# Pairing two early softmax tiles of an attention and MLP kernel: when their exponentials run

## The chip, the cores and the metric

The kernel runs on one core of one Trainium2 chip. The metric is the device time of one execution in microseconds (us); less is better. The time before is 385.89 us, the median of 3 runs (385.85 to 385.94).

The engines named below are PE (TensorE, matrix products; PEld is its load of weights), DVE (VectorE), ACT (ScalarE), POOL (GpSimd) and SP (SyncE, which here does nothing but issue DMAs). Each engine takes its instructions strictly in the order in which the program gives them, so an instruction that waits holds up all that stand behind it on its engine.

## The reference

One transformer block over 2048 positions of width 576: an attention in which each position looks at itself and at seven earlier positions two apart, with 32 heads of 18 channels, and a two-layer MLP with 4608 hidden channels. Both have a layer norm ahead and a residual behind.

```python
def _A_ref(x, wqkv, wo):                       # H = 32, Dh = 18, W = 8, dil = 2
    qkv = (x @ wqkv).reshape(B, S, 3, H, Dh)   # then transposed to q, k, v
    idx = pos[:, None] - off[None, :]          # off = 0, 2, ..., 14
    mask = idx >= 0
    logits = jnp.einsum("bhsd,bhswd->bhsw", q, kg) * scale
    logits = jnp.where(mask[None, None, :, :], logits, -1e9)
    attn = _softmax(logits, axis=-1)
    o = jnp.einsum("bhsw,bhswd->bhsd", attn, vg)
    return o.transpose(0, 2, 1, 3).reshape(B, S, D) @ wo
def _B_ref(x, w1, b1, w2, b2):
    y = _layernorm(x, axis=-1)
    h = _gelu(jnp.einsum("bsd,df->bsf", y, w1) + b1)   # tanh form
    return jnp.einsum("bsf,fd->bsd", h, w2) + b2
x = A_x
h = x + _A_ref(_layernorm(x, axis=-1), A_wqkv, A_wo)
h2 = h + _B_ref(_layernorm(h, axis=-1), B_w1, B_b1, B_w2, B_b2)
return h2
```

## The kernel before

**Tiles and groups.** The 2048 positions are cut into 16 tiles of 128 (numbers n = 0 to 15). Two neighbouring tiles make a group (g = 0 to 7): the MLP runs a group at a time, the attention a tile at a time. In this text "tile 2" is n = 2, the third tile.

**A list scheduler in Python sets the order.** Every piece of work is a task with an engine, an estimated cost, the tasks it comes after, a priority and, where it needs one, a buffer slot (class Weaver, L16). `run()` keeps an estimated clock for each engine and takes, again and again, the ready task with the earliest estimated start; among tasks with the same start the lower priority number goes first (L58). An engine's instruction order is the order in which its tasks are taken; it is fixed before the kernel runs. Loads on SP also carry an estimate of the DMA queue: 240 KB per us (L33), and a task that waits for a load starts, in the plan, at that landing. A change to one dependency can therefore move any task behind it, on all engines.

**The tasks of one tile**, with the names that the prediction uses:

- `c{n}Q/K/V` (PE, L392): the three projections, each 10 matmuls; `e{n}Q/K/V` (ACT, L405): their eviction from PSUM. K and V go into one slot of an eight-slot window (`kwin`, `vwin`); even and odd positions have a window each.
- `p1a`, `p1s`, `p1t`, `p1b` (DVE, L444, L450, L457 to L463), together the logits of a tile: q times the K window, a tree of adds, then maximum and subtraction. The tile's product uses the single buffer `prod`.
- `ex{n}` (ACT, L467): the exponential over the tile's logits, in place.
- `p2n` (DVE, L437 to L439, L475, L478): the sum, its reciprocal and the weights; `p2a`, `p2s`, `p2b` (DVE, L485, L491, L495 to L497): the weights times the V window and a tree of adds. `p2a` uses `prod` too.
- `ks{n}`, `vs{n}` (SP, L519, L521): once tile n's logits (or its product with V) have read the window, one slot of K (of V) is loaded again from DRAM, shifted by one row, for the next tile. `p1a` of a tile waits for the `ks` of all earlier tiles of its parity, `p2a` for their `vs`.
- `t2{n}`: the transposes of the attention's output. For tiles 0 to 2 they are nine PE transposes into a PSUM buffer (`t2p`, L321) and a copy by ACT (L538); from tile 3 on two DMA transposes (L540, L541).
- `wo{n}` (PE, L563): the output projection; `woe{n}` (ACT, L568): its eviction; `xr{n}` (SP, L572): the residual is loaded.
- `ln2a`, `hb` (DVE, L576, L306, L307, L310, L589): residual, statistics of the second layer norm, and the residual plus the last bias; `ln2r` (POOL, L314): the reciprocal root; `ln2m` (DVE, L584); `ln2b` (ACT, L593): the normalized tile; `t3{n}`: its transposes into `hnT`, by PE and ACT or by DMA in the same way as `t2`.

**The MLP of group g** is a row of nine units. `u{g}.{u}` (PE, L629) is 36 matmuls into one PSUM buffer `pm`; `g{g}.{u}` (ACT, L640) is the four gelus that empty it. After the row `m{g}.…` (PE, L666) multiplies by w2 in four passes, and `out` (DVE, L685) adds the residual. A unit of row g comes after both `t3` of its group and after the last `m` of the group before.

**PSUM.** There are three `pm` buffers. Projections, PE transposes, output projections and units of all rows share them; each is free again when ACT has emptied it.

**ACT's tables.** Exponential and gelu use different activation tables; a table load (ACT_TABLE_LOAD) stands in the program wherever one follows the other. Copies, casts and `Identity` do not bring a load about.

**Where the exponentials stand before.** For tiles 6 to 15 (groups 3 to 7) both tiles of a group get their logits first; both exponentials come after that and after the last gelu of the group two before, and ahead of the first gelu of the group before (L509, L651). For tiles 0 to 5 each exponential comes after its own tile's logits and may fall anywhere. Logits of tile 4 and later may start once the logits of the tile before are done; those of tiles 1, 2 and 3 wait until the tile before is through with its product with V (L501).

Of the kernel before, what the change touches and what calls it, by code (L numbers as in the profile page):

```python
# [15 lines left out]
class Weaver:  # L16
# [9 lines left out]
    def add(self, name, engine, cost, fn, after=(), prio=0.0, take=None, give=(), lag=0.1, table=None, kb=0.0,  # L26
            backlog=2.5, transfers=1):
        assert name not in self.tasks, name
        self.tasks[name] = (engine, cost, fn, tuple(after), prio, take, tuple(give), lag, table,
                            (kb, backlog, transfers))  # L30
# [60 lines left out]
def kernel(  # L91
# [33 lines left out]
    GROUPS = [[n, n + 1] for n in range(0, NT, 2)]  # L125
# [47 lines left out]
    add = wv.add  # L173
# [41 lines left out]
    UN = FH // 2  # L215
# [19 lines left out]
    Q, K, V = 0, 1, 2  # L235
# [194 lines left out]
    def attention(n):  # L430
        j = ORDER[n]
        e, s = j % 2, j // 2
# [60 lines left out]
        def p2b():  # L493
# [4 lines left out]
                                    op=ALU.add)  # L498

        ready = [f"e{m}K" for m in same] + [f"ks{m}" for m in before]  # L500
        add(f"p1a{n}", "DVE", 2.65, p1a, ready + [f"e{n}Q"] + [f"lg{n}"] + ([f"p2b{n - 1}"] if 0 < n < 4 else [f"p1b{n - 1}"] if n else []), prio=n,  # L501
            take=("prod", f"prod{n}"), give=(f"q{n}",))
        add(f"lg{n}", "-", 0.0, lambda: None, [f"lg{n - 1}"] if n else [], take=("lg", f"lg{n}"), lag=0.0)
        add(f"p1s{n}", "DVE", 1.37, lambda: p1b(((9, 18),)), (f"p1a{n}",), prio=n)
# [1 line left out]
        add(f"p1b{n}", "DVE", 1.75, p1c, (f"p1t{n}",), prio=n - 1, give=(f"prod{n}",))  # L506
        g, _ = group_of[n]

        gate = [f"p1b{m}" for m in GROUPS[g]] + [f"g{g - 2}.{UN - 1}"] if g >= 3 else [f"p1b{n}"]  # L509
        add(f"ex{n}", "ACT", 0.45, ex, gate, prio=-50, table="exp")  # L510
        ready = [f"e{m}V" for m in same] + [f"vs{m}" for m in before]
        add(f"p2n{n}", "DVE", 1.35, p2n, [f"ex{n}"] + ([f"p2a{n - 1}"] if n else []), prio=-8 + n, give=(f"lg{n}",))
# [103 lines left out]
    def mlp(g):  # L616
# [3 lines left out]
        def unit(u):  # L620
            def fn():
                pm = ps_pm.tile([P, 2, 2, 256], F32, tag="pm", name="pm")
                T["pm", g, u] = pm
                for q in range(2):
                    f0 = (2 * u + q) * P
                    for c in range(KC):
                        for half in range(2):
                            lo = 64 * half
                            nc.tensor.matmul(pm[:, half, q, 0:width], lhsT=w1_sb[lo:lo + 64, c, f0:f0 + P],  # L629
                                             rhs=T["hnT", g][lo:lo + 64, block(c, half), 0:width],  # L630
                                             start=(c == 0), stop=(c == KC - 1))
            return fn

        def gelu(u):
            def fn():
                T["hT", g, u] = late_pool().tile([P, 2, 2, 256], BF16, tag="hT", name="hT", bufs=HT)
                for q in range(2):
                    for half in range(2):
                        ft = half * FH + 2 * u + q
                        nc.scalar.activation(out=T["hT", g, u][:, half, q, 0:width],  # L640
                                             in_=T["pm", g, u][:, half, q, 0:width],
                                             func=ACT.Gelu_apprx_tanh, bias=b1_sb[:, ft:ft + 1])
            return fn
# [3 lines left out]
        for u in range(UN):  # L647
            deps = [f"t3{n}" for n in ns] + ["b1e"] + w1s[2 * u * P // CW] + w1s[(2 * u + 1) * P // CW] + last
            add(f"u{g}.{u}", "PE", cost, unit(u), deps + ([f"u{g}.{u - 1}"] if u else []), prio=100 + 20 * g,
                take=("pm", f"pm{g}.{u}"), lag=0.3)  # L650
            exps = [f"ex{n}" for n in GROUPS[g + 1]] if u == 0 and 2 <= g < len(GROUPS) - 1 else []  # L651
            add(f"g{g}.{u}", "ACT", 4 * (0.17 + width * 0.8e-3), gelu(u), [f"u{g}.{u}"] + exps + (qkv_done if g + u == 0 else []), prio=0,
                take=("hT", f"hT{g}.{u}"), table="gelu",
                give=(f"pm{g}.{u}",) + ((f"hnT{g}",) if u == UN - 1 else ()))
        passes = [(a, half) for a in range(len(ns)) for half in range(2)]
        for i, (a, half) in enumerate(passes):
            n = ns[a]
# [36 lines left out]
    for n in range(NT):  # L694
        front(n)
        attention(n)
        project(n)
    for g in range(len(GROUPS)):
        mlp(g)
# [32 lines left out]
```

## Time and profile before

| quantity | value |
|---|---|
| median of 3 runs | 385.89 us |
| the profiled execution's own time | 385.97 us |
| its span in the trace | 384.2 us |
| ACT busy | 213.7 us (56%) |
| DVE busy | 292.1 us (76%) |
| granted TensorE clock | 1.0 |
| exponentials (L467) | 16, of 0.42 us (median) |
| table loads ahead of an exponential / of a gelu | 8 / 9, of 1.283 us each |
| exponentials start at | 30.77, 46.16, 63.09, 82.25, 91.87 and 114.82 us (tiles 0 to 5), then in pairs at 143.27, 179.38, 217.13, 254.87 and 292.84 us |
| first gelu, last gelu of row 0 | 79.37 us, ends at 101.0 us |
| DVE in slices of the span | 80% or more busy in nearly all of 10 to 280 us |

The span is what the profiler saw of the execution; 1.8 us of the time lie around it. Times inside the trace are counted from the span's start. "Idle" of an engine is told with the instruction that ended it. The chain of waits is followed back from the last instruction: at each step to whatever released it.

### The profile page before, as it was taken

What the parts mean: (1) busy time and instruction counts of PE and PEld (TensorE: products, weight loads), DVE (VectorE), ACT (ScalarE), POOL (GpSimd) and SP (SyncE); (2) the same over time, 40 slices, a digit from 0 to 9 for tenths busy, and PEclk for the clock granted to TensorE, in tenths of its full rate; (3) what the DMA queues carried; (4) which work ended last, traced back from release to release, by engine and by line L of the source; (5) the groups of instructions that cost most, each with busy time, mean ns of one, the idle gap of its engine ahead of it and who ended that gap; (6) DMA issues with size and microseconds to landing.
All of it is one profiled execution on the core that took longest, in us unless ns stands there. A gap on an engine that the chain in (4) does not pass through costs nothing.

```text
span 384.2 us, 10767 instructions
## 1 busy us (share of the span) xinstructions
PE 374.3 (97%) x4618; PEld 305.8 (80%) x4618; DVE 292.1 (76%) x563; ACT 213.7 (56%) x441; POOL 32.5 (8%) x55
## 2 busy tenths in 40 slices
PE   7999999997999999999999999999999999999996
PEld 3777787786878887888788878887887788778874
DVE  7999999999999999999999899989964942010000
ACT  2796675899535781477148804870586068206700
POOL 3660011010011010011001100110010011000000
PEclk9999999999999999999999999999999999999999
DMA  8889999987332211322342323413331321100000
GB/s 253 252 183 262 210 234 236 312 258 220 84 79 64 64 32 32 96 49 48 77 80 52 59 73 97 50 38 89 80 33 32 92 50 33 32 15 19 2 16 16
DMA packets 63967, 38.48 MB, mean 100 GB/s; under 512 B 39520, under 2 KB 63904, under 8 KB 63920
## 3 DMA queue, kind: packets, MB, share of 16 engines
q1 hardware_dynamic: 63296, 37.13, 40.6%
q8 instruction: 36, 0.59, 0.7%
q10 hardware_dynamic: 624, 0.66, 0.5%
q14 instruction: 11, 0.09, 0.1%
HBM read 22.28 MB, written 6.52 MB: 75 GB/s over the span
## 4 chain that ended last, share of the span: by engine, by line
PE 87%; DVE 5%; ACT 5%; POOL 1%; issue 1%
PE po L666 37%; PE pm L629 34%; PE pq L392 11%; PE pw L563 5%; DVE l_st L306 3%; ACT hT L640 2%; POOL l_rs L314 1%; DVE l_mv L307 1%; ACT L640 1%; ACT L467 1%; DVE kwin L349 1%; PE pt L321 1%; ACT hn L593 0%; DVE l_ve L310 0%; POOL nmr L344 0%
## 5 line engine op out<-in xcount | busy, mean ns | idle before, releaser
L640 ACT ACTIVATE hT<-pm,b_sb 128x256 bf16<-128x256 f32 x288 | 112.1, 483 | 109.0 <-PE pm L629 109.0
L629 PE MATMUL pm<-hnT,w_sb 64*128 64x256 bf16 x2592 | 145.2, 269 | 2.7 <-ACT hT L640 2.7
L666 PE MATMUL po<-w_sb,hT 128*128 128x288 bf16 x1152 | 143.0, 286 | 0.0
L629 PEld LDWEIGHTS <-w_sb 64*128 64x128 bf16 x2592 | 126.6, 94 | 19.2 <-issue 4.7
L666 PEld LDWEIGHTS <-hT 128*128 128x128 bf16 x1152 | 111.9, 98 | 30.2 <-issue 2.2
L685 DVE TENSOR_TENSOR osb<-po,hb 128x288 bf16<-128x288 f32 x32 | 14.3, 452 | 53.8 <-PE po L666 53.7
L314 POOL TENSOR_TENSOR l_rs<-l_ve,mhalf 128x1 f32<-128x1 f32 x32 | 27.1, 846 | 282.6 <-DVE l_ve L310 281.9
L450 DVE TENSOR_TENSOR prod<-prod 128x2304 bf16<-128x2304 bf16 (+1 forms) x64 | 44.1, 689 | 1.6
L485 DVE TENSOR_TENSOR prod<-vwin,at 128x4608 bf16<-128x4608 bf16 x16 | 40.8, 2553 | 0.4 <-ACT vwin L405 0.2
L444 DVE TENSOR_TENSOR prod<-kwin,q 128x4608 bf16<-128x4608 bf16 x16 | 40.8, 2553 | 0.3
L392 PE MATMUL pq<-wqkv_sb,vwin 128*128 128x288 bf16 x210 | 27.5, 286 | 1.4 <-ACT vwin L368 0.8
L392 PE MATMUL pq<-wqkv_sb,kwin 128*128 128x288 bf16 x210 | 27.1, 286 | 0.0
L392 PEld LDWEIGHTS <-vwin 128*128 128x128 bf16 x210 | 20.1, 98 | 7.0 <-ACT vwin L368 1.4
L593 ACT ACTIVATE hn<-h,nmr,l_rs 128x576 bf16<-128x576 f32 (+1 forms) x32 | 19.2, 654 | 11.1 <-DVE nmr L584 8.5
L392 PEld LDWEIGHTS <-kwin 128*128 128x128 bf16 x210 | 20.2, 98 | 5.4 <-issue 0.5
L491 DVE TENSOR_TENSOR prod<-prod 128x2304 bf16<-128x2304 bf16 x16 | 21.7, 1358 | 0.5
L563 PE MATMUL pw<-wo_sb,oT 64*128 64x288 bf16 x288 | 20.3, 283 | 0.0
L576 DVE TENSOR_TENSOR h<-h,xr 128x576 f32<-128x576 f32 x16 | 12.0, 752 | 10.5 <-ACT h L568 10.5
L563 PEld LDWEIGHTS <-oT 64*128 64x128 bf16 x288 | 13.6, 94 | 4.3 <-issue 1.2
L437 DVE TENSOR_TENSOR half<-lg 128x128 f32<-128x128 f32 x32 | 9.2, 289 | 9.0 <-ACT lg L467 8.4
L405 ACT CAST kwin<-pq 128x576 bf16<-128x576 f32 x16 | 10.2, 639 | 6.9 <-PE pq L392 6.9
L405 ACT CAST vwin<-pq 128x576 bf16<-128x576 f32 x16 | 10.2, 641 | 6.4 <-PE pq L392 6.3
(63 smaller groups left out, 231.5 us busy)
## 6 DMA issues: line engine op xcount, KB each, us to landing
w_sb<-in_B_w_dram SPq DMA_DIRECT2D x36, 288.0 KB, 5.5
xr<-in_A_x_dram SPq DMA_DIRECT2D x16, 144.0 KB, 2.4
out_dram<-osb SPq DMA_DIRECT2D x16, 144.0 KB, 1.9
kvd<-kwin SPq DMA_DIRECT2D x14, 144.0 KB, 4.2
kvd<-vwin SPq DMA_DIRECT2D x14, 144.0 KB, 3.4
kwin<-kvd SPq DMA_DIRECT2D x14, 144.0 KB, 2.5
vwin<-kvd SPq DMA_DIRECT2D x14, 144.0 KB, 2.2
wqkv_sb<-in_A_wqkv_dram SPq DMA_DIRECT2D x4, 288.0 KB, 5.0
```

Source lines behind the costliest of these rows:

```text
L314: nc.gpsimd.tensor_tensor(out=L["rs"][:, n, :], in0=L["ve"][:, n, :], in1=mhalf[:], op=ALU.pow)
L392: nc.tensor.matmul(pq[:, p0:p0 + HALF], lhsT=T["xnT", n][:, kt, :], rhs=wqkv_sb[:, kt, c0:c0 + HALF], start=(kt == 0), stop=(kt == KT - 1))
L405: nc.scalar.copy(out=dst.rearrange("p (d h) -> p d h", h=H), in_=src.rearrange("p h d -> p d h"))
L444: nc.vector.tensor_tensor(out=prod[:], in0=kwin[e][:], in1=T["q", n][:].unsqueeze(1).to_broadcast([P, W, D]), op=ALU.mult)
L450: nc.vector.tensor_tensor(out=pv[:, :, 0:b - a, :], in0=pv[:, :, 0:b - a, :], in1=pv[:, :, a:b, :], op=ALU.add)
L485: nc.vector.tensor_tensor(out=prod[:].rearrange("p w (d h) -> p w d h", d=Dh, h=H), in0=vwin[e][:].rearrange("p w (d h) -> p w d h", d=Dh, ...
L491: nc.vector.tensor_tensor(out=prod[:, 0:4, :], in0=prod[:, 0:4, :], in1=prod[:, 4:8, :], op=ALU.add)
L563: nc.tensor.matmul(pw[:, half, 0:HALF], lhsT=T["oT", n][lo:lo + 64, block(c, half), :], rhs=wo_sb[lo:lo + 64, c, :], start=(c == 0), stop= ...
L593: nc.scalar.activation(out=hn_slots[n % 2][:, c0:c1], in_=src, func=ACT.Identity, scale=L2["rs"][:, n, :], bias=nmr[:, n, :])
L629: nc.tensor.matmul(pm[:, half, q, 0:width], lhsT=w1_sb[lo:lo + 64, c, f0:f0 + P], rhs=T["hnT", g][lo:lo + 64, block(c, half), 0:width], st ...
L640: nc.scalar.activation(out=T["hT", g, u][:, half, q, 0:width], in_=T["pm", g, u][:, half, q, 0:width], func=ACT.Gelu_apprx_tanh, bias=b1_s ...
L666: nc.tensor.matmul(T["po", n, half][:], lhsT=T["hT", g, u][:, r, q, a * P:(a + 1) * P], rhs=w2_sb[:, ft, half * HALF:(half + 1) * HALF], s ...
```

## The change

Three conditions in the scheduler's input change. No instruction of the arithmetic is added, removed or resized.

1. `p1a3`, the first step of tile 3's logits, no longer comes after `p2b2` (tile 2's last step with V) but after `p1b2` (the end of tile 2's logits), as tiles 4 to 15 have it already.
2. The gate of the exponentials: for every group but the first, both tiles' logits must be done (before: from group 3 on); from group 2 on also the last gelu of the group two before (before: from group 3 on). So `ex2` and `ex3` come after `p1b2` and `p1b3`; `ex4` and `ex5` after `p1b4`, `p1b5` and `g0.8`.
3. The first gelu of a row comes after the next group's two exponentials for every row but the last (before: from row 2 on). So `g0.0` comes after `ex2` and `ex3`, and `g1.0` after `ex4` and `ex5`.

```diff
-        add(f"p1a{n}", "DVE", 2.65, p1a, ready + [f"e{n}Q"] + [f"lg{n}"] + ([f"p2b{n - 1}"] if 0 < n < 4 else [f"p1b{n - 1}"] if n else []), prio=n,
+        add(f"p1a{n}", "DVE", 2.65, p1a, ready + [f"e{n}Q"] + [f"lg{n}"] + ([f"p2b{n - 1}"] if 0 < n < 3 else [f"p1b{n - 1}"] if n else []), prio=n,
...
-        gate = [f"p1b{m}" for m in GROUPS[g]] + [f"g{g - 2}.{UN - 1}"] if g >= 3 else [f"p1b{n}"]
+        gate = [f"p1b{m}" for m in GROUPS[g]] if g else [f"p1b{n}"]
+        gate += [f"g{g - 2}.{UN - 1}"] if g >= 2 else []
         add(f"ex{n}", "ACT", 0.45, ex, gate, prio=-50, table="exp")
...
-            exps = [f"ex{n}" for n in GROUPS[g + 1]] if u == 0 and 2 <= g < len(GROUPS) - 1 else []
+            exps = [f"ex{n}" for n in GROUPS[g + 1]] if u == 0 and g < len(GROUPS) - 1 else []
             add(f"g{g}.{u}", "ACT", 4 * (0.17 + width * 0.8e-3), gelu(u), [f"u{g}.{u}"] + exps + (qkv_done if g + u == 0 else []), prio=0,
```

## The prediction, made before the changed kernel had run

> **What bounds the kernel now.** I read the page's busy shares first, then the chain of waits, then the timelines of PE and ACT where the chain leaves PE.
>
> ```profile
> PE 374.3 (97%) x4618; PEld 305.8 (80%) x4618; DVE 292.1 (76%) x563; ACT 213.7 (56%) x441; POOL 32.5 (8%) x55
> ```
>
> PE works 374.3 of 384.2 us; ten are left to win. In stages of the span, PE idles under 0.3 us in all of 28.8 to 77.36 us, and nothing that matters from 99.33 to the end. One stage is different, the row of gelus of group 0. The chain, in order of time (start, us, what):
>
> ```profile
> 76.15 1.21 PE pw L563 x18
> 77.36 1.98 PE pm L629 x36
> ...
> 95.22 4.11 PE pm L629 x72
> 99.33 3.05 PE po L666 x24
> ...
> 345.17 17.79 PE pm L629 x324
> ```
>
> The last row (345.17) shows what nine units cost without a stall: 17.79 us for 324 matmuls. Row 0 runs from 77.36 to 99.33, 21.97 us, with only one other thing between its units (nine transposes, 0.50). So 21.97 - 0.50 - 17.79 = **3.68 us** are lost there. PE's timeline has the holes:
>
> ```profile
> 77.20 8.02 PE L629 MATMUL pm<-hnT,w_sb 64*128 64x256 bf16 x144
> 85.60 2.14 PE L629 MATMUL pm<-hnT,w_sb 64*128 64x256 bf16 x36 [0.38 <-ACT hT L640]
> 88.14 0.66 PE L321 MATMUL pt<-ident,hn 128*128 128x128 bf16 x9 [0.40 <-ACT hT L640]
> 89.60 4.11 PE L629 MATMUL pm<-hnT,w_sb 64*128 64x256 bf16 x72 [0.80 <-ACT hT L640]
> 95.22 4.11 PE L629 MATMUL pm<-hnT,w_sb 64*128 64x256 bf16 x72 [1.51 <-ACT hT L640]
> ```
>
> 0.38 + 0.40 + 0.80 + 1.51 = 3.09 us of idling, each until ACT's gelus had freed a pm buffer; the other 0.6 us are the pipe filling again after each stop (four times about 0.15). Why ACT is late is in its own timeline:
>
> ```profile
> 79.37 1.57 ACT L640 ACTIVATE hT<-pm,b_sb 128x256 bf16<-128x256 f32 x4
> 80.96 1.28 ACT L467 ACT_TABLE_LOAD   x1
> 82.25 0.42 ACT L467 ACTIVATE lg<-lg 128x256 f32<-128x256 f32 x1
> 82.68 1.28 ACT L640 ACT_TABLE_LOAD   x1
> ...
> 89.37 1.19 ACT L538 COPY hnT<-pt 128x1152 bf16<-128x1152 bf16 x1
> 90.58 1.28 ACT L467 ACT_TABLE_LOAD   x1
> 91.87 0.42 ACT L467 ACTIVATE lg<-lg 128x256 f32<-128x256 f32 x1
> 92.30 1.28 ACT L640 ACT_TABLE_LOAD   x1
> ```
>
> Tile 3's exponential (82.25) and tile 4's (91.87) split the row; each brings two loads. That is 4 x 1.30 + 2 x 0.42 = 6.0 us of ACT, and ACT is busy 21.77 of the stage's 21.97 us. ACT bounds this stage alone.
>
> **The change, part by part.**
>
> *Removed.* Four table loads and two exponentials leave row 0. In their place come tile 2's t2 copy (1.12, the row at 73.77) and woe2 (0.64), since tile 2 is finished later; ln2b2 (1.20) and the hnT copy (1.19) now in the row move out of it for the same reason. ACT's load is then 21.77 - 6.0 - 2.4 + 1.8 = 15.2 us, against PE's 17.79 + 0.50 + 1.21 = 19.5. ACT no longer bounds. The loads go from 8 and 9 to 6 and 7. Gain: up to 3.68.
>
> *The wait of ex2, ex3 for p1b3.* One tile's logits cost DVE 7.4 us (72.69 to 80.1), its second half 1.65 + 5.4 = 7.0 (96.83 to 103.9), ln2a with hb 2.6 (80.01 to 82.63). p1b2 ends at 63.06; ln2a1 and hb1 are ready and go first, to 65.65; tile 3's logits then end at 65.65 + 7.4 + 0.2 (L584) = 73.2. Both exponentials are through at 73.9. Behind them on ACT stand the last evictions, for which PE's projections wait; if the plan's DVE runs ahead of the real one, PE feels it. At 63.09 ex2 started at once behind the eviction, with no wait, so I cost this at nothing; without that cover it is a us for each us of drift beyond the three pm buffers.
>
> *The wait of g0.0 for ex2, ex3.* t2 (0.50) and wo (1.21) of tile 2 leave the time before row 0, so its first unit starts at 77.36 - 1.71 = 75.65 and ends at 77.6. The last eviction, some 0.65 after the projections, is through at 76.3, the gelu table at 77.6. The exponentials are 3.7 us early. Nothing.
>
> *Moved into the row: t2, wo of tile 2.* Same work, but the transposes hold a pm buffer until ACT copies them. Row 1 has an output projection and its eviction amid its units, and comes to 11.90 + 1.10 + 5.89 = 18.89, which is 17.79 + 1.10: no stall. So 0 from that row, and at most the whole copy, 1.12, from the other side; I take 0.4, nearer to row 1, as ACT has some 0.4 us to spare per unit (1.57 against 1.97).
>
> A rule speaks against this step. The Trainium skill, Perfetto Trace Analysis, in Optimization Strategy, reads an engine's repeated gap as perhaps too little SBUF or PSUM for the next tile. By it the pm ring would be at fault, two more users in it would keep the holes, and the time would stay near 386; the row at 345.17, which runs on the same three buffers without a hole, is on the other side.
>
> *DVE's order.* When p1b3 ends, p2n2 must wait for the exponential, and p1a4 is ready; in the trace p1a4 (82.63) slipped in the same way while ex3 was out. So: logits 4 to 80.6, then tile 2's and tile 3's second halves: p2b3 ends at 73.2 + 7.4 + 7.0 + 7.0 = 94.6 (before: 96.9). If ln2a2 comes ahead of it, 97.2. p1b5 then ends at about 94.6 + 2.6 + 7.4 + 2.6 = 107.2 (before 114.7).
>
> *What is late next: tile 3.* Row 1 needs t3 of tile 3. Before, from p2b3 (96.9) to the second hnT transpose (issued at 112.33, 2.5 to landing) took 17.9 us. After: 94.6 + 17.9 = 112.5, or 115.1. PE wants row 1 at 75.65 + 17.79 + 0.50 + 1.21 (tile 2) + 0.50 (its t3) + 18.08 (m of group 0: 3.05 + 7.08 + 7.95) + 1.21 (wo3) = 114.94; wo4 falls behind it. Cost 0 to 0.2; I take 0.
>
> *The wait of ex4, ex5 for p1b5 and g0.8.* g0.8 is through near 95, so p1b5 decides. ex4 and ex5 run from 107.2 to 107.9; ln2b3 and the gelu table stand behind them on ACT: 107.9 + 1.2 + 1.28 = 110.4, before 114.94. Nothing; uncovered, tile 3's transposes are late by as much.
>
> *DMAs.* On SP, ks3 moves up from 75.28 to about 68.2 and vs2 with xr2 back from 69.84 to about 84.5; four DMAs of tile 2 and 3 in all, none added. Behind vs2 stand chunks of w2. The last w2 chunk was issued by 89.0 and chunks land in 5.4, at 94.4; the m of group 0 start at 95.2 and use the last chunk some 4 us later. Nothing from that row; each us that SP is held beyond it costs up to one.
>
> *The sum.* 385.97 (profiled) - 3.68 + 0.4 = 382.69; the median of the runs is 0.08 lower: **382.6**. Its own range: 381.9 (nothing exposed, and the 0.33 by which group 0's m exceed the usual 17.75) to 383.6 (the copy exposed, 0.2 at row 1).
>
> **Rivals.**
>
> *Tile 3 is put behind tile 5 (slower, 388).* p2a3 needs vs2, issued when p2a2 ends; between lie p2s2, p2b2 and p2n3, 1.36 + 1.4 + 1.65 = 4.4 us (in the plan's costs 4.07). The window loads of V took a median of 2.9 us in 28 to 65 us and 3.3 in 65 to 100, with the DMA engines near full there; in the plan a load takes 0.4 + 0.61 + 1.8, and a w2 chunk ahead adds up to 1.2. If the plan has vs2 land after p2n3, p1a5 is ready and is taken, and with prod in its hands it holds p2a3 up by 7.4, with ln2a2 by 10: p2b3 at 104.6, t3 of tile 3 at 122.5, and PE stands 7.6 us at row 1, less 1.21 for wo4, 6.4. Time 382.6 + 6.4 = 389.0; 387 if ln2a2 doesn't add to it. It costs from p2b3 = 97.0 on, and the kernel is slower than before once p2b3 passes 100.3. For it: the margin of some 0 to 1 us in a loaded queue. Against: ranking by priority (p2a3 -5, p1a5 5) when both are ready.
>
> *A part is given back (384.3).* p2b3 at 97 to 99, exponentials ahead of ln2b3, or w2 late behind SP's wait for vs2: 1 to 2.5 us of stall, 383.6 to 385.1. For it: the margins of 2.4 and 0.8 us just worked out. Against: each errs on the safe side of the trace's rows.
>
> *The holes stay (385.9).* Table loads go but the t2 copy and woe2 block the ring as the exponentials did. Against: 15.2 us of ACT against 19.5 of PE.
>
> **How the numbers follow.** Forecast 0.60, part given back 0.13, holes stay 0.06, tile 3 behind tile 5 0.21. About 0.2% (0.8 us) is what a measurement of this kernel tells from no change, so faster ends at 385.1 and slower starts at 386.7: faster 0.60 + 0.13 less 0.01 at the edge = 0.72, same 0.07, slower 0.21. The range goes from 381.8 to 387.0: it leaves out a few chances in a hundred below and most of the slower case above. The likeliest case's own range is 381.9 to 383.6.
>
> **What would show it.** Right: no table load between g0.0 and g0.8; exponentials in pairs near 73 and 107 us; PE's idle until ACT in row 0 falls from 3.09 to under 0.5; row 1 starts near 115. Wrong: an idle PE ahead of row 1 until the hnT transposes, with L444 of tile 5 ahead of L485 of tile 3; ACT waiting for DVE before 75 us with PE idle behind it; PE waiting for w2 at the start of group 0's m.

## The result, and the profile after

The changed kernel takes 382.79 us (median of 4 runs, 382.47 to 382.88) against 385.91 us before (4 runs on the same chip): ratio 0.9916, 95% interval 0.9899 to 0.9933. It is 3.1 us faster. The forecast was 382.6 us. The profiled execution took 382.82 us, its span is 381.0 us; both are compared below with 385.97 and 384.2 before. In this document a ratio is a time over that of the kernel before, with its 95% interval.

The page's busy shares: PE works as much as before, in a shorter span; ACT lost 4.7 us and four instructions, the table loads.

```profile
PE 373.8 (98%) x4618; PEld 304.8 (80%) x4618; DVE 292.5 (77%) x563; ACT 209.0 (55%) x437; POOL 32.4 (9%) x55
```

ACT's timeline of the changed kernel, from the exponentials of tiles 2 and 3 to those of tiles 4 and 5 (start, us, engine, line, operation; idle before it in brackets):

```profile
72.84 0.75 ACT L467 ACTIVATE lg<-lg 128x256 f32<-128x256 f32 x2
...
75.99 1.28 ACT L641 ACT_TABLE_LOAD   x1
77.41 1.57 ACT L641 ACTIVATE hT<-pm,b_sb 128x256 bf16<-128x256 f32 x4
...
89.20 1.57 ACT L641 ACTIVATE hT<-pm,b_sb 128x256 bf16<-128x256 f32 x4 [0.40 <-PE pm L630]
90.64 1.13 ACT L539 COPY oT<-pt 128x1152 bf16<-128x1152 bf16 x1
91.88 1.57 ACT L641 ACTIVATE hT<-pm,b_sb 128x256 bf16<-128x256 f32 x4
...
105.62 1.28 ACT L467 ACT_TABLE_LOAD   x1
106.92 0.72 ACT L467 ACTIVATE lg<-lg 128x256 f32<-128x256 f32 x2
```

Both pairs of exponentials stand outside the row. ACT now waits for PE (0.40 us ahead of most units), where PE waited for ACT. PE's timeline of the same stretch:

```profile
75.23 13.93 PE L630 MATMUL pm<-hnT,w_sb 64*128 64x256 bf16 x252
89.09 0.68 PE L321 MATMUL pt<-ident,o 128*128 128x128 bf16 x9
89.70 4.10 PE L630 MATMUL pm<-hnT,w_sb 64*128 64x256 bf16 x72
93.64 1.27 PE L564 MATMUL pw<-wo_sb,oT 64*128 64x288 bf16 x18
94.84 7.03 PE L667 MATMUL po<-w_sb,hT 128*128 128x288 bf16 x56
101.80 1.28 PE L564 MATMUL pw<-wo_sb,oT 64*128 64x288 bf16 x18
103.67 0.79 PE L321 MATMUL pt<-ident,hn 128*128 128x128 bf16 x9 [0.59 <-ACT hn L594]
104.29 10.94 PE L667 MATMUL po<-w_sb,hT 128*128 128x288 bf16 x88
115.16 6.07 PE L630 MATMUL pm<-hnT,w_sb 64*128 64x256 bf16 x108
```

Row 0 has no hole left, even with tile 2's transposes and output projection in it. One new wait stands behind the row: 0.59 us until ACT has tile 2's normalized rows. The chain of waits shows where that wait comes from, some 30 us earlier (start, us, what):

```profile
65.62 2.47 DVE prod L444
68.12 5.73 DMA kwin<-kvd
73.87 2.56 DVE prod L444
...
102.74 0.88 ACT hn L594
103.62 0.05 issue
103.67 0.79 PE pt L321 x9
```

The load `ks3` of the K window, issued when tile 3's product had read it, took 5.73 us to land. DVE stood 0.94 us for it ahead of tile 4's product, and what stands behind it on DVE, tile 2's second layer norm too, came later by it; the second profile of this kernel, further down, confirms that.

Where the time went, by the chains of both kernels, each stretch less the pieces that only one of them has in it: up to the start of group 0's second matmuls 98.83 against 94.91 us (the hnT transposes' 0.50 taken off before), **3.92 won**, about 3.6 of it in the row and 0.3 ahead of it, where PE had waited 0.16 us for an eviction; from there to row 1 19.28 against 19.82, 0.54 lost (the new wait and its refill, less 0.33 since the matmuls are cut up less often); from row 1 to the end 0.27 lost, most of it output projections that now stand between matmuls of `po`, where they cost 1.21 instead of 1.10. Together 3.11 of the span.

### The profile page after: what moved, and what is told of

Same layout as the page of the kernel before. It is cut to its first block, busy times and chain, and to the rows that moved or that the text cites. A ratio compares the mean times of both kernels' runs of the same rounds, so it can differ in the third digit from the quotient of the medians.

```text
span 381.0 us, 10766 instructions
## 1 busy us (share of the span) xinstructions
PE 373.8 (98%) x4618; PEld 304.8 (80%) x4618; DVE 292.5 (77%) x563; ACT 209.0 (55%) x437; POOL 32.4 (9%) x55
## 4 chain that ended last, share of the span: by engine, by line
PE 72%; DVE 14%; DMA 2%; issue 1%; POOL 0%; ACT 0%; DVEq 0%; ACTq 0%
PE po L667 35%; PE pm L630 33%; PE pw L564 4%; DVE prod L444 3%; DVE prod L450 2%; DVE prod L485 2%; DMA kwin<-kvd 2%; DVE prod L491 1%; DVE l_st L306 1%; DVE prod L495 1%; DVE h L577 1%; DVE half L437 0%; DVE half L438 0%; DVE hb L590 0%; DVE lg L457 0%
## 5 line engine op out<-in xcount | busy, mean ns | idle before, releaser
L641 ACT ACTIVATE hT<-pm,b_sb 128x256 bf16<-128x256 f32 x288 | 112.5, 477 | 88.6 <-PE pm L630 88.3
L569 ACT COPY h<-pw 128x576 f32<-128x576 f32 x16 | 10.5, 654 | 15.4 <-PE pw L564 15.4
```

## The experiments

Two of the three edits can be judged from the scheduler alone. The first by itself (`p1a3` after `p1b2`) gives, on every engine, the very instruction order of the kernel before: the scheduler takes tile 2's second half first by its priority. The changed kernel without the third edit (gelus behind the next pair's exponentials) has the very instruction order of the changed kernel. What acts is the second edit, the gate of the exponentials; the first is needed with it, as `ex2` would otherwise wait for logits that wait for `ex2`.

**Table loads put back into row 0.** The question: is it ACT's time in the row, or the new order of tiles 2 and 3, that brings the gain?

```diff
+    spare = wpool.tile([P, 16], F32, name="spare")
...
                                              func=ACT.Gelu_apprx_tanh, bias=b1_sb[:, ft:ft + 1])
+                if g == 0 and u in (0, 4):
+                    nc.scalar.activation(out=spare[:], in_=b1_sb[:, 0:16], func=ACT.Exp)
```

> The changed kernel with an exponential of 128x16 values, whose result nobody uses, behind units 0 and 4 of row 0: four table loads are back in the row, and nothing else moves. Theory: 4 x 1.3 + 2 x 0.2 = 5.6 us more on ACT, 20.8 against PE's 19.5 in the row: 384.2 to 385.9. Rival 1 (order): 382.8.

Measured: 386.02 us (12 runs, ratio 0.9985, 0.9971 to 0.9999), 0.1 above the theory's band, but in two clusters: five runs at 384.38 to 384.41 and seven at 385.98 to 386.60. The profiled one is of the second; there PE idles 2.09 us in one piece, and then its clock falls (last section):

```profile
92.20 5.77 PE L631 MATMUL pm<-hnT,w_sb 64*128 64x256 bf16 x72 [2.09 <-ACT hT L642]
```

The first cluster, with a mean clock of 0.998 or more, is taken as the cost of the loads: 384.4 - 382.8 = 1.6 us. It lies in the theory's band, and rival 1 falls: the order of the tasks is the same on every engine and the time is not.

**The same time on ACT without a table load.** The gelus of units 0 and 4 are done three times.

```diff
-                for q in range(2):
+                for q in [0, 1] * (3 if g == 0 and u in (0, 4) else 1):
```

> The changed kernel with the gelus of units 0 and 4 of row 0 done three times: 16 more activations, some 5.9 us more on ACT, no table load. Theory (it is ACT's time that counts, whatever it is spent on): as with the exponentials in the row, within 0.5 us of that run. Rival 2 (a table switch costs more than its row shows, through a drain): 0.5 to 3 us faster than the run with the exponentials.

Measured: 384.33 us (5 runs, 384.31 to 384.90; ratio 0.9959, 0.9947 to 0.9971), 0.1 us from the first cluster of the run with exponentials. PE's timeline of it has the holes of the kernel before again:

```profile
75.22 6.07 PE L630 MATMUL pm<-hnT,w_sb 64*128 64x256 bf16 x108
81.94 8.04 PE L630 MATMUL pm<-hnT,w_sb 64*128 64x256 bf16 x144 [0.65 <-ACT hT L641]
90.68 0.66 PE L321 MATMUL pt<-ident,o 128*128 128x128 bf16 x9 [0.71 <-ACT hT L641]
92.14 4.11 PE L630 MATMUL pm<-hnT,w_sb 64*128 64x256 bf16 x72 [0.80 <-ACT hT L641]
```

0.65 + 0.71 + 0.80 = 2.16 us, and group 0's second matmuls start at 97.28 instead of 94.84. Of these 2.44 us, row 1 sees 1.69 (116.85 against 115.16), because the later PE no longer waits for tile 2's rows. So a load is worth its row on ACT and nothing more, and rival 2 falls: the two runs, with 5.6 and 5.9 us more on ACT by their rows, take the same time. The Trainium skill (ScalarE: Activation LUTs, What ACT_TABLE_LOAD costs) counts 1.28 us of load and 1.38 us of drain for each switch; four switches would then cost 10.6 us of ACT, an estimate from that page. The load is confirmed here (1.283 us in every row), the drain is not seen.

The two runs give back less than the whole gain, and the rows say why (from and to, length, then busy times and instructions of PE, PEld, DVE, ACT and POOL, the granted clock of TensorE, the busy share of the DMA engines and GB/s). The first row is the kernel before, the second the changed one, the third the run with the gelus:

```profile
77.36:99.33 21.97, 18.88 (x335) 17.20 (x331) 20.72 (x43) 21.77 (x43) 0.99 (x1) 1.00 0.70 218
...
75.35:94.84 19.49, 19.49 (x352) 16.88 (x348) 18.11 (x30) 16.44 (x38) 0.00 (x0) 1.00 0.78 242
...
75.35:97.40 22.05, 19.90 (x352) 18.54 (x349) 20.64 (x32) 21.63 (x55) 0.00 (x0) 1.00 0.78 243
```

ACT is as full in the third row (21.63 of 22.05 us) as in the first (21.77 of 21.97). But the third has 1.21 us more of PE's own work in it, tile 2's output projection, which fills time in which PE would have waited. That is the 1.2 us between the 3.6 won in the row and the 2.44 given back. This account is read from the rows; no run takes the projection out of the row.

**Only tiles 2 and 3 paired.** Tile 4's exponential then falls behind unit 1 of row 0.

```diff
-        gate = [f"p1b{m}" for m in GROUPS[g]] if g else [f"p1b{n}"]
-        gate += [f"g{g - 2}.{UN - 1}"] if g >= 2 else []
+        gate = [f"p1b{m}" for m in GROUPS[g]] if g and g != 2 else [f"p1b{n}"]
+        gate += [f"g{g - 2}.{UN - 1}"] if g >= 3 else []
...
-... if u == 0 and g < len(GROUPS) - 1 else []
+... if u == 0 and g != 1 and g < len(GROUPS) - 1 else []
```

> Only tiles 2 and 3 are paired; tile 4's exponential falls behind unit 1 of row 0 with its two table loads. Theory: ACT in row 0 has 15.2 + 3.0 = 18.2 us of work against PE's 19.5, but it comes in one lump of 3.0 us against three pm buffers: holes of 0.3 to 1.2 us, 383.0 to 384.2. Rival 1 (order of tile 2): all of the gain, 382.8 or less.

Measured: 385.14 us (8 runs, 384.60 to 385.50; ratio 0.9976, 0.9966 to 0.9986), 0.9 above the theory's band and far from rival 1. The row itself is as the theory had it: one hole of 0.77 us, group 0's second matmuls 1.16 later. Another 0.60 came behind the row: PE waits 1.19 us for tile 2's rows instead of 0.59. Some 0.2 more go with group 0's second matmuls, which are cut into four pieces instead of two. The last 0.2 of the 2.2 us between the two profiles stay unexplained.

**Only tiles 4 and 5 paired.**

```diff
-... if 0 < n < 3 else ...
+... if 0 < n < 4 else ...
-        gate = [f"p1b{m}" for m in GROUPS[g]] if g else [f"p1b{n}"]
+        gate = [f"p1b{m}" for m in GROUPS[g]] if g >= 2 else [f"p1b{n}"]
...
-... if u == 0 and g < len(GROUPS) - 1 else []
+... if u == 0 and 1 <= g < len(GROUPS) - 1 else []
```

> Only tiles 4 and 5 are paired; tile 3's exponential stays in row 0, tile 2 is transposed and projected ahead of the row as before. Theory (ACT's time for the two exponentials with their table loads, 3.0 us each, starves PE of pm buffers): the hole that tile 4's exponential made (1.51 us and its refill) goes, those behind tile 3's (0.38, 0.40, 0.80) stay mostly: 383.8 to 384.8. Rival 1 (the gain is that tile 2's layer norm and hnT copy left row 0, or DVE's new order): nothing gained, 385.9.

Measured: 387.76 us (5 runs, 387.73 to 388.38; ratio 1.0051, 1.0039 to 1.0063). Both expectations missed: it is slower than the kernel before. Row 0 did what the theory said, the 1.51 us hole is gone and group 0's second matmuls start at 97.97 instead of 99.26. But more is lost behind it. ACT's timeline:

```profile
99.66 1.28 ACT L467 ACT_TABLE_LOAD   x1
100.96 0.42 ACT L467 ACTIVATE lg<-lg 128x256 f32<-128x256 f32 x1
104.90 0.42 ACT L467 ACTIVATE lg<-lg 128x256 f32<-128x256 f32 x1 [3.52 <-DVE lg L463]
105.22 0.62 ACT L569 COPY h<-pw 128x576 f32<-128x576 f32 x1
...
112.60 1.20 ACT L594 ACTIVATE hn<-h,nmr,l_rs 128x576 bf16<-128x576 f32 x2 [6.76 <-DVE nmr L585]
```

Tile 5's exponential waits 3.52 us for its logits, and tile 3's eviction (L569), whose product PE had finished by 103.7, stands behind it. It misses its turn on DVE, where tile 6's product goes first, and tile 3's normalized rows come at 112.60 instead of 109.41. PE waits for them and, later, for DVE's output adds:

```profile
PE po L667 <- DVE osb L686: 2.5, 2, 1.4
...
PE pm L630 <- DMA hnT<-hn: 1.0, 1, 1.0
```

So in these runs the pair (4, 5) pays only with the pair (2, 3) ahead of it: there both exponentials start 1.3 us after the table load does, and here the second one 5.2 after it.

**The prediction's slower rival, forced.** One dependency puts tile 3's product with V behind tile 5's logits.

```diff
-        add(f"p2a{n}", "DVE", 2.57, p2a, ready + [f"p2n{n}"] + ([f"p2b{n - 1}"] if n else []), prio=-8 + n,
+        add(f"p2a{n}", "DVE", 2.57, p2a, ready + [f"p2n{n}"] + (["p1b5"] if n == 3 else []) + ([f"p2b{n - 1}"] if n else []), prio=-8 + n,
```

> The changed kernel with one dependency more: tile 3's product with V comes after tile 5's logits. This forces the order of the prediction's slower rival and asks for its price. Theory: p2b3 falls from 95.4 to about 105, the hnT transposes of tile 3 land near 122, and PE, which wants row 1 near 115, stands 5 to 7 us: 387 to 390. Rival (row 1 has slack that the chain doesn't show): under 385.

Measured: 390.83 us (4 runs, 390.18 to 391.07; ratio 1.0124, 1.0110 to 1.0138), 0.8 above the theory's band and 8.0 above the changed kernel, where 6.4 were worked out. `p2b3` ends at 102.6, the second hnT transpose of tile 3 is issued at 118.94, PE's row 1 is held in two steps:

```profile
120.12 0.28 PE L630 MATMUL pm<-hnT,w_sb 64*128 64x256 bf16 x2 [1.51 <-DMA hnT<-hn]
121.47 7.63 PE L630 MATMUL pm<-hnT,w_sb 64*128 64x256 bf16 x106 [1.07 <-DMA hnT<-hn]
```

Further waits are 1.78 us for an output add that stands behind tile 3's product and tile 2's layer norm on DVE, 0.83 for tile 4's transposes and 1.33 for a gelu. Behind the holes at row 1 the clock of PE falls (stretches of 2 us, columns as above):

```profile
122.00:124.00 2.00, 2.00 (x24) 1.71 (x22) 1.93 (x5) 0.00 (x0) 0.00 (x0) 0.52 0.51 146
124.00:126.00 2.00, 2.00 (x28) 1.78 (x26) 1.90 (x6) 1.20 (x4) 0.44 (x1) 0.63 0.36 82
```

By the two rows that is 2 x 0.48 + 2 x 0.37 = 1.7 us of full clock lost; the other 6.3 are close to the price that was worked out. The rival was real. Its waits were priced right in their sum and not in their places, since one wait of 7.6 us at row 1 was worked out and 2.58 stand there. The clock made it dearer.

**Tiles transposed by DMA.** With PE busy from end to end, less PE work should be time. First both transposes of tile 2 go this way, then those of tiles 1 and 2 (`TO = 1`), then all (`TO = 0`).

```diff
-    TP, TO = 8, 3
+    TP, TO = 8, 2
```

> The changed kernel with tile 2's two transposes by DMA, as tiles 3 to 15 have them: 18 matmuls less on PE (2 x 0.50 us), two copies less on ACT (1.13 + 1.12), and PE no longer waits for tile 2's normalized rows before its transposes (0.59). Theory (PE's own work and waits are the time): 382.8 - 1.0 - 0.6 = 381.2, if tile 2's hnT lands before row 1, near 114. Rival (the DMA way is some 5 us longer for each transpose and pushes tile 2 behind tile 3): 1 to 4 us of stall ahead of row 1, 382 to 385.

Measured: 383.90 us (5 runs, 383.43 to 384.64; ratio 0.9952, 0.9939 to 0.9966), slower than the changed kernel. The rival's band, but not its mechanism. PE's waits:

```profile
PE po L667 <- DMA w_sb<-in_B_w_dram: 1.4, 3, 1.0
```

The first transpose of tile 2 waits on SP until tile 2 is through with its product with V (88.3), and w2 chunks stand behind it; the last one is issued at 98.62 instead of 93.90.

> The same for tiles 1 and 2: 36 matmuls less on PE, 2.0 us. Theory: 380.2, if tile 1's hnT lands before row 0, which is wanted near 74. Rival (DMA queues are near full before 95 us and tile 1 comes late): row 0 starts late by 1 to 5 us, 381 to 386.

Measured: 389.09 us (4 runs; ratio 1.0081, 1.0068 to 1.0095), outside of both bands; w2 alone holds PE for 2.26 us at a stretch, and behind that the clock falls to 0.50.

> All transposes of the attention's and the layer norm's output by DMA: 54 matmuls less on PE, 3.0 us. Theory: 379.2 if tiles 0 to 2 are all in time. Rival: tile 0's DMAs come amid the loads of weights and hold SP up; as for tiles 1 and 2 or worse, 380 to 386.

Measured: 399.41 us (4 runs; ratio 1.0357, 1.0342 to 1.0372), outside of both bands too; w2 holds PE 4.8 us at a stretch, the transposes 4.5. These two add to the first only that the losses grow.

**Only t3 of tile 2 by DMA**, behind the w2 chunks on SP.

```diff
-            if n < TO:
+            if n < (TO if key == "t2" else 2):
```

> The changed kernel with only t3 of tile 2 by DMA; its t2 stays on PE, so that no DMA transpose stands ahead of the last w2 chunks on SP. Nine matmuls less on PE (0.50) and no wait for tile 2's normalized rows (0.59, and some 0.15 of refill). Theory: that wait is all that the changed kernel still loses around rows 0 and 1, and w2's lateness in the run with both transposes by DMA came from t2's place on SP: 381.5 to 381.9. Rival (tile 2's DMAs delay tile 3's, which row 1 waits for): 382.3 or more.

Measured: 383.21 us (5 runs, 383.00 to 383.79; ratio 0.9930, 0.9918 to 0.9943). The rival's band. PE's work shrank and its wait for tile 2 is gone, and the next wait took their place (PE's timeline):

```profile
114.54 6.37 PE L630 MATMUL pm<-hnT,w_sb 64*128 64x256 bf16 x108 [0.56 <-DMA hnT<-hn]
```

Row 1 could now start at 114.0 and waits for tile 3's hnT until 114.5. The changed kernel starts it at 115.2: it has at most 0.7 us to spare there. Two chains, PE's work and DVE's chain from tile 4's product to tile 3's rows, are nearly equally long.

**The changed kernel again**, on the chip of the run before:

> The changed kernel as it is, on the same chip: 382.5 to 382.9.

Measured: 382.23 us (4 runs, 382.14 to 382.77; ratio 0.9907, 0.9892 to 0.9923). That is 0.3 below the lowest time expected and 0.6 faster than the first four runs. The trace says why:

```profile
73.21 2.56 DVE L444 TENSOR_TENSOR prod<-kwin,q 128x4608 bf16<-128x4608 bf16 x1 [0.28 <-DMA kwin<-kvd]
```

`ks3` landed 0.66 us sooner, DVE was 0.66 us earlier behind it, PE did not wait for tile 2's rows at all, and the execution took 382.19 instead of 382.82 us.

**w2 behind ks3.** Two w2 chunks are issued at 65.0, shortly ahead of `ks3`. Here no w2 chunk goes out before it.

```diff
-        bulk(f"w2{c}", w2_chunk(c), 295, prio=30 + c, after=("b2", "b1t", "warm"))
+        bulk(f"w2{c}", w2_chunk(c), 295, prio=30 + c, after=("b2", "b1t", "warm", "ks3"))
```

> The changed kernel with every w2 chunk behind ks3, so that the two chunks issued at 65.0 no longer stand ahead of ks3 (68.12) in the DMA engines. Theory: ks3 lands in under 5 us, DVE doesn't wait for it (0.3 to 0.9 before), and PE's wait of up to 0.59 for tile 2's normalized rows is gone; but two chunks less are in by 68, the last w2 chunk goes out behind ks5, near 99, and PE waits for it by 0.5 to 1.5 us in the m of group 0: 382.5 to 383.5. Rival (w2 has room): 382.1 or less.

Measured: 384.21 us (5 runs, 384.20 to 384.26; ratio 0.9955, 0.9942 to 0.9969). The part on `ks3` holds: no load of the K window takes over 4.3 us, and DVE waits for none, so the two chunks ahead of it were what delayed it: in all nine profiles that have them, `ks3` takes 5.1 to 6.0 us. The price was larger than worked out (the theory's band ended at 383.5), and of another kind. PE's waits:

```profile
PE pw L564 <- DMA oT<-o: 1.4, 1, 1.4
...
PE po L667 <- DMA w_sb<-in_B_w_dram: 0.3, 1, 0.3
```

The scheduler, which sees tile 3 earlier, put its output projection ahead of more of group 0's matmuls, and its transposes were not there yet.

> The changed kernel once more, on the same chip: 382.1 to 382.9, by how long ks3 takes to land.

Measured: 382.66 us (4 runs, 381.88 to 383.10; ratio 0.9913, 0.9899 to 0.9926). The profiled execution took 383.10: `ks3` landed after 6.0 us and DVE waited 1.18. PE waited 0.47 for a w2 chunk, and after that only 0.15 for tile 2's rows; tile 2's transposes start 0.23 later than in the first profile (103.90), as tile 4's product did (74.10).

No version beats the changed kernel. A fourth pm buffer was not tried.

## Why the prediction was right

*Row 0's loss, 3.68.* This term was right. The row with tile 2's transposes (0.50) and projection (1.21) in it takes 19.49 us, PE busy for all of them; 17.79 + 0.50 + 1.21 = 19.50. ACT is busy 16.4 us there, 1.2 more than the 15.2 worked out, and still under PE: gelus that had run behind the row's end, until 101.0, now run inside it. (The sum of 15.2 also has a slip: `woe2` was added as new, but it stood in that stretch before, at 77.40. An eviction of 0.64 at 75.33 makes up for it.)

*That ACT's time in the row is the cause.* Shown by the two runs that put it back, with and without table loads. They restore 2.44 us of the 3.6 won in the row, and 1.5 to 1.6 of the whole 3.1. The rest of the row's gain is argued from the rows and not run.

*The wait of ex2, ex3 and g0.0.* This was right too. `p1b3` ended at 72.9 (worked out: 73.2), the exponentials at 73.6 (73.9), row 0 started at 75.4 (75.65), and ACT did not wait for DVE.

*0.4 for tile 2's pieces in the row.* The amount of the allowance was about right and its place was wrong. The pieces cost nothing in the row. What was lost, 0.54, is the new wait at 103.67, from a step that the prediction had costed at nothing: the **DMAs**. "Nothing from that row" was taken for w2 and `vs2`; `ks3`, moved up by 7 us into the busiest stretch of the DMA engines and directly behind two weight chunks, took 5.1 to 6.0 us where K window loads before took 2.5 in the median and 3.7 at most. The prediction named its new place and did not price it. That the sum still came within 0.2 us is in part luck: 0.3 won ahead of the row, 0.27 lost behind row 1 and this 0.54 stood in no term, and together they come to 0.5, near the 0.4 allowed.

*What is late next.* The times were close: `p2b3` 95.4 (94.6), `p1b5` 106.0 (107.2), row 1 115.2 (114.94). The margin was not: 2.4 us were given to tile 3's hnT. In the changed kernel its second transpose is issued at 111.89 and lands 3.1 us later, at 115.0. From `p2b3` to that landing are 19.6 us, not 17.9: DVE comes to tile 3's layer norm 1.1 us later, and the landing takes 3.1 instead of 2.5. So 0.2 us are left by this trace, and at most 0.7 by the run with one transpose less on PE.

*w2.* The last chunk was given as issued by 89.0, from the kernel before; in the changed one SP is held by `vs3` until 92.56, and it is issued by 94.4. In two of the three profiles that was early enough. In the third PE waited 0.47 for a chunk, in time in which it would otherwise have waited for tile 2's rows.

*The rivals.* "Tile 3 behind tile 5" did not come about, since `vs2` was in the plan's time; forced, it costs 8.0 us where 6.4 stood, and 1.7 of them are a fallen clock. (Its milder form, given as 387, comes to 386.4 by the same sum: 102.0 + 17.9 - 114.94 - 1.21 = 3.75 over 382.6.) "A part is given back" happened on a small scale, by the DMA and not by what it named first. "The holes stay" did not come about, with the same three `pm` buffers.

## What to carry to other kernels

Where the bound engine idles in one stage of many, compare that stage with the same work elsewhere in the trace: the difference is about what a repair can bring there (3.68 us here, of which 3.1 were left at the end). The engine to relieve is the one that is full in that stage, however idle it is on average. And a step that is moved takes its loads with it: the price of a load is that of its new neighbours, not of the row it left, so look up what will be in the queues there.

## What the runs showed of the hardware

**A hole of some 2 us can cost as much again by the clock, and need not.** In the profiled run with the exponentials in row 0, PE idles 2.09 us in one piece. The stretches around it (columns as above; the granted clock is the third number from the right):

```profile
90.00:92.00 2.00, 0.11 (x2) 0.09 (x1) 1.97 (x2) 1.99 (x5) 0.00 (x0) 1.00 0.58 185
92.00:94.00 2.00, 1.80 (x26) 1.70 (x27) 1.97 (x2) 2.00 (x6) 0.00 (x0) 0.80 0.21 47
94.00:96.00 2.00, 2.00 (x23) 1.76 (x20) 1.83 (x5) 1.26 (x3) 0.00 (x0) 0.50 1.00 284
96.00:98.00 2.00, 2.00 (x34) 1.91 (x32) 2.00 (x1) 0.92 (x3) 0.00 (x0) 0.85 0.38 133
```

By the rows 1.7 us of full clock are lost (2 x 0.20 + 2 x 0.50 + 2 x 0.15), close to the distance between the run's two clusters, 384.4 and 386.0. Five of the twelve executions had a mean clock of 0.998 or more, the other seven 0.991 to 0.996; only one, of the seven, was profiled.

The length of a hole does not decide it alone. In the tiles 1 and 2 run a hole of 2.26 us is followed by a clock of 0.50, but in the run with all transposes by DMA two holes of 2.10 and 2.43 us have a clock of 1.00 behind them. In the run with tile 5 ahead a hole of 1.78 us at 105.6 has 1.00 behind it, and three shorter ones within 5 us (0.83, 1.51 and 1.07) are followed by the fall. Holes of 1.51 us and less had a full clock in the profile of the kernel before. Nor does a low mean clock have to come from a hole in the row: in the profile of the tiles 4 and 5 run the clock is 0.50 from 8 to 10 us, behind start-up waits of 1.00 and 0.79 us. What else decides stays open.

**The changed kernel's time follows single DMA landings.** Its twelve runs lie between 381.88 and 383.10 us, where most of those of the kernel before lie within 0.1 us of each other. Its three profiled executions go with `ks3`: DVE waits for it of 0.28, 0.94 and 1.18 us belong to 382.19, 382.82 and 383.10 us.
